# Linear attention and squared-ReLU FFN on one core: a new written-out issue order, W1 in eighths, transposes by TensorE or DMA chosen per unit

## The chip, the core and the metric

The kernel runs on one core of one Trainium2 chip. The metric is device time in microseconds (us); ten runs of the kernel before have a median of 180.53 us (179.64 to 183.67). The profile is that of one execution of 180.4 us, whose recorded span is 178.6 us. The engines are called PE (matrix engine), DVE (vector), ACT (scalar), POOL (GpSimd) and SP (the queue that issues most transfers).

## The reference

```python
# r, k, v: (4, 8, 768, 48) float32; w, u: (8, 48)
for t in range(S):
    cur = einsum('bhd,bhe->bhde', u * k[t], v[t])
    y[t] = einsum('bhd,bhde->bhe', r[t], state + cur)
    state = w[..., None] * state + einsum('bhd,bhe->bhde', k[t], v[t])
x = y.transpose(0, 2, 1, 3).reshape(3072, 384)
h = maximum(x @ w_in, 0)          # w_in: (384, 2048)
out = (h * h) @ w_out             # w_out: (2048, 384)
```

A decaying state per head and batch gives y, and all 3,072 tokens then go through a feed-forward layer whose hidden values are squared after the ReLU.

## The kernel before, in words

The sequence is cut into 24 *units* of 128 tokens; unit i is chunk i // 4 of batch i % 4. Units are taken together in 13 *groups* for the feed-forward layer: units 0 and 1 alone, then pairs (group 5 holds units 8 and 9, group 7 units 12 and 13).

Every operation is a *step* with a short name, a method of the class `Do`. A unit needs these:

- `ld` loads r, k and v as float32, from rows of 48 values (five buffers for each of r, k and v).
- `kh` and `rh` multiply k and r by powers of the decay (`Wkhat`, `Wt2`) into the bf16 tile `rk`; `vb` casts v to bf16. `P0`, `P1`, `du` and `dv` make the term of the current token: r * k, times u, summed over the head, times v.
- `rk` has to be transposed: `T` on PE into a PSUM bank and `Tc` that copies it out, or `XB`, one DMA transpose issued by SP. `A` multiplies the transposed tiles, `Bm` applies the causal mask while it moves the product out of PSUM.
- `Y` adds up the chunk's own part and the state's; `xs` moves it out of PSUM and adds `dv`. `U` makes the update of the state, `ts` and `S` (for the first chunks `S0`) apply it to `S0W`.
- `xs` has to be transposed as well: `X` on PE and `xTc`, or `xX`, a DMA transpose on SP.

A group then needs `F1` (eight steps per pair: 6 matmuls of 256 columns; for a single unit four steps of 12 matmuls of 128 columns), `re` (ReLU out of PSUM), `sq` (the square: form 0 on ACT, form 1 multiplies the PSUM bank by the ReLU's result, form 2 the result by itself out of SBUF), and per unit four `F2` steps of 4 matmuls of 384 columns, one for each quarter of W2. `os` evicts, `out` stores.

The weights: W1 is loaded in float32 quarters by SP (`lW`, L301) and cast to bf16 by `cW`; W2 comes in quarters by `W` (L317), a casting DMA issued by POOL. Ahead of each `W`, a `gate` (L311) copies one value of a v tile on POOL, so that the DMA is issued only after that tile has landed.

The string `ORDER` is the whole program: steps with their engine (A, D, G, P, S for ACT, DVE, POOL, PE, SP) and the buffers they take, worked out ahead of time and walked once by the loop at the end of the function. Each engine runs its steps strictly in that order, and waits where a step's input or buffer isn't ready. So the engine of a step, and its place among that engine's other steps, are what the string decides.

Of the kernel before, what the change touches and what calls it, by code (L numbers as in the profile page):

```python
# [29 lines left out]
sq.1.1:D2/3 ld.r.7:S/2 re.0.3:A/4 Bm.3.1:D/3 P0.3:G/3 F2.1.0:P/0 re.0.0:A/5 sq.0.3:D1/4 Y.2:P/0 ld.v.11:S/3  # L30
sq.0.0:A0/5 P0.4:G/1 F1.0.1:P/1 Bm.3.0:D/2 WLcol:A F2.0.0:P/1 xs.2:D/2 re.0.1:A/1 gate.1.3:G Y.3:P/2 W.1.3:G P1.3:D
X.2:P/0 sq.0.1:A0/6 F1.0.2:P/0 du.3:D/1 WLm:G xTc.2:A/0 re.0.2:A/0 F2.1.1:P dv.3:G S0.1:D sq.0.2:A0/7 U.3:P/0 S0.0:D
F2.0.1:P ld.r.6:S/3 rh.4:G xs.3:D/0 U.2:P/1 S0.3:D X.3:P/3 P1.4:G T.4:P/2 xTc.3:A S0.2:D F2.1.2:P Tc.4:A/4 kh.5:D/5
F1.2.1:P/1 du.4:D/0 F1.2.5:P/0 re.2.1:A/3 dv.4:G A.4:P/0/3 re.2.5:A/2 sq.2.1:D1/8 F2.0.2:P sq.2.5:A0/9 ld.k.10:S/4
kh.6:G/0 Bm.4.1:D/0 F2.1.3:P Bm.4.0:D/1 ld.v.5:S/4 F1.2.7:P/0 os.1:A/0 F1.2.3:P/1 ld.k.11:S/3 re.2.7:D/4 vb.9:A/5
Y.4:P/1 re.2.3:A/5 U.4:P/2 ld.v.6:S/1 rh.5:D F1.2.0:P/0 sq.2.3:A0/10 ts.4:D/0 P0.5:G/0 T.5:P/3 out.1:S sq.2.7:A0/11
xs.4:D/1 F1.2.6:P/1 S.4:G Tc.5:D/5 ld.r.9:S/4 re.2.0:A/1 X.4:P/0 F2.0.3:P sq.2.0:A0/12 re.2.6:D/0 ld.k.8:S/0 P1.5:G
A.5:P/2/1 vb.11:A/6 xTc.4:D/1 F2.2.0:P/0 ld.v.7:S/2 Bm.5.1:D/5 sq.2.6:A0/13 rh.6:G F1.2.4:P/0 os.0:A/1 du.5:D/2
ld.r.11:S/0 F1.2.2:P/1 Bm.5.0:D/4 re.2.4:A/3 kh.7:G/1 out.0:S F2.3.0:P/1 vb.5:A/7 re.2.2:D/2 T.6:P/3 dv.5:G
sq.2.4:D1/14 sq.2.2:A0/15 Y.5:P/0 U.5:P/1 Tc.6:A/0 F2.2.1:P rh.7:D ld.v.10:S/4 xs.5:D/2 P0.6:G/2 F2.2.2:P vb.6:A/0  # L40
ts.5:D/1 X.5:P/2 F2.2.3:P P0.7:G/3 ld.k.9:S/1 xTc.5:A ld.r.12:S/3 T.7:P/3 os.2:A/2 F1.3.1:P/1 P1.6:D ld.k.12:S/2
Tc.7:A/1 ld.r.8:S/2 F1.3.5:P/0 du.6:D/1 P1.7:G out.2:S re.3.1:D/5 vb.7:A/3 A.6:P/0/1 A.7:P/2/3 S.5:G re.3.5:A/4
du.7:D/0 F2.3.1:P sq.3.5:A0/16 Bm.6.0:D/2 F2.3.2:P dv.7:G sq.3.1:A0/17 Bm.6.1:D/3 F1.3.7:P/1 vb.10:A/1 Bm.7.0:D/1
kh.8:G/4 F1.3.0:P/0 ld.v.8:S/2 re.3.7:A/1 Y.6:P/0 sq.3.7:A0/18 dv.6:D F1.3.3:P/1 re.3.0:A/0 xs.6:D/0 kh.9:G/2
ld.v.12:S/1 U.6:P/1 F2.3.3:P re.3.3:D/3 sq.3.0:A0/19 X.6:P/2 rh.8:G F1.3.2:P/0 ts.6:D/0 os.3:A/0 sq.3.3:A0/20 out.3:S
F2.4.0:P/0 S.6:D XB.8:S/2 re.3.2:A/2 F1.3.4:P/1 Bm.7.1:D/0 P0.8:G/1 sq.3.2:A0/21 F1.3.6:P/0 re.3.4:D/4 xTc.6:A/0
P1.8:G F2.4.1:P ld.k.13:S/0 sq.3.4:D1/22 re.3.6:A/5 ld.r.13:S/2 Y.7:P/0 vb.8:A/4 sq.3.6:D1/23 rh.9:G F2.4.2:P
vb.12:A/2 xs.7:D/1 U.7:P/1 F2.4.3:P P0.9:G/0 XB.9:S/3 ts.7:D/1 X.7:P/3 F2.5.0:P/1 os.4:A/1 S.7:D xTc.7:A ld.k.14:S/1
F2.5.1:P out.4:S du.8:D/2 P1.9:G F1.4.5:P/1 ld.r.14:S/4 F1.4.1:P/0 dv.8:D re.4.5:A/1 F2.5.2:P du.9:D/1 kh.10:G/3
ld.v.13:S/2 sq.4.5:A0/24 F1.4.3:P/1 re.4.1:A/0 dv.9:D AA.8:P/2/0/1/3 sq.4.1:A0/25 rh.10:G re.4.3:D/3 ld.v.14:S/0  # L50
F1.4.4:P/0 Bm.8.0:D/4 sq.4.3:A0/26 F1.4.0:P/1 P0.10:G/2 XB.10:S/4 Bm.8.1:D/5 re.4.4:A/2 F2.5.3:P sq.4.4:A0/27
re.4.0:D/4 P1.10:G ld.k.15:S/4 Y.8:P/2 vb.13:A/7 ld.r.15:S/1 U.8:P/0 os.5:D/2 F1.4.7:P/0 sq.4.0:A0/2 kh.11:G/5
xs.8:D/2 out.5:S F1.4.2:P/1 re.4.7:A/5 ts.8:D/0 xX.8:S/1 F2.6.0:P/0 rh.11:G Bm.9.0:D/2 sq.4.7:A0/5 F1.4.6:P/0
re.4.2:A/1 Bm.9.1:D/3 S.8:G XB.11:S/5 F2.7.0:P/1 sq.4.2:A0/3 du.10:D/0 Y.9:P/2 re.4.6:A/0 dv.10:D U.9:P/0 F2.7.1:P
sq.4.6:A0/6 xs.9:D/0 P0.11:G/3 ld.v.15:S/4 F2.7.2:P ts.9:D/1 vb.14:A/0 xX.9:S F2.7.3:P P1.11:G ld.k.16:S/3 ld.r.16:S/0
F2.6.1:P os.7:D/0 S.9:G AA.10:P/1/3/2/0 du.11:D/2 out.7:S F2.6.2:P vb.15:A/3 dv.11:D F1.5.0:P/1 Bm.10.0:D/1 kh.12:G/0
ld.v.16:S/3 F1.5.1:P/0 Bm.10.1:D/0 re.5.0:A/3 rh.12:G F2.6.3:P Bm.11.0:D/4 re.5.1:A/2 Y.10:P/1 sq.5.0:D1/0 sq.5.1:A0/7
P0.12:G/1 XB.12:S/0 U.10:P/3 F1.5.2:P/0 os.6:A/1 xs.10:D/1 F1.5.3:P/1 P1.12:G vb.16:A/4 ld.k.17:S/2 ts.10:D/0 out.6:S
re.5.2:A/4 F2.8.0:P/1 Bm.11.1:D/5 xX.10:S/0 S.10:G re.5.3:A/5 F2.9.0:P/0 ld.r.17:S/3 sq.5.2:D1/1 sq.5.3:A0/4 Y.11:P/2
du.12:D/1 kh.13:G/1 U.11:P/1 F1.5.4:P/1 xs.11:D/2 F1.5.5:P/0 ts.11:D/1 rh.13:G re.5.4:A/1 F2.8.1:P re.5.5:A/0 dv.12:D  # L60
XB.13:S/1 F2.9.1:P sq.5.5:A0/12 xX.11:S S.11:G sq.5.4:D1/8 F1.5.6:P/0 ld.v.17:S/1 F1.5.7:P/1 P0.13:G/0 re.5.6:A/2
F2.8.2:P re.5.7:A/3 sq.5.6:D1/15 P1.13:G ld.k.18:S/0 F2.9.2:P sq.5.7:A0/10 ld.r.18:S/2 AA.12:P/3/0/2/1 kh.14:G/4
du.13:D/0 F2.8.3:P dv.13:D F1.6.0:P/1 vb.17:A/5 Bm.12.0:D/2 rh.14:G os.8:A/2 ld.v.18:S/2 F1.6.1:P/0 re.6.0:A/4 out.8:S
Bm.12.1:D/3 F2.9.3:P P0.14:G/2 re.6.1:A/5 XB.14:S/2 sq.6.0:D1/14 Y.12:P/3 os.9:A/0 U.12:P/0 F1.6.2:P/0 Bm.13.0:D/1
P1.14:G sq.6.1:A0/9 ld.k.19:S/1 out.9:S F1.6.3:P/1 xs.12:D/0 re.6.2:A/0 ld.r.19:S/4 kh.15:G/2 ts.12:D/0 F2.10.0:P/1
# [12 lines left out]
Bm.17.0:D/4 F2.13.2:P vb.21:A/7 sq.8.0:D1/27 Y.16:P/1 re.8.1:A/3 P1.18:G ld.k.23:S/0 U.16:P/3 F2.13.3:P ld.r.23:S/2
sq.8.1:A0/24 xs.16:D/1 kh.19:G/1 F1.8.2:P/0 ts.16:D/0 vb.22:A/0 xX.16:S/1 Bm.17.1:D/5 os.13:A/1 F1.8.3:P/1 S.16:G
# [443 lines left out]
```

## Time and profile before

| | |
|---|---|
| median of ten runs | 180.53 us |
| profiled execution, and its span | 180.4 us, 178.6 us |
| PE, DVE, ACT, POOL busy | 157.6, 124.8, 119.9, 113.9 us |
| F1 matmuls (L433), F2 matmuls (L460) | 74.5 us busy, 73.3 us busy |
| one load of r, k or v | 192 KB, 3.7 to 4.0 us from issue to landing |
| one quarter of W2 | 7.7 us from issue to landing |
| one transpose by DMA of rk, of xs | 3.4 us, 3.1 us from issue to landing |

Busy time is the union over an engine's instructions, so overlapping matmuls aren't counted twice. A group's row has its number of instructions, their busy time, the mean of one, and the idle time of the engine ahead of them with what ended it. The chain of waits is followed back from the last instruction, and shows which work or wait set the end.

### The profile page before, as it was taken

Reading aid. Unit: us, or ns where it says so; the run is one execution under the profiler, and the core shown is the slowest. Engines: PE = TensorE matmul, PEld = TensorE weight load, DVE = VectorE, ACT = ScalarE, POOL = GpSimd, SP = SyncE. Lnnn points to the kernel's source line nnn. Section 1 sums busy time; section 2 is a strip of 40 time slices with the busy share of each in tenths; the row PEclk is TensorE's granted clock in tenths of the full one; section 3 lists DMA queues with packets and bytes.
Section 4 is the critical chain, followed back from the end, with each engine's and each line's share of the span. In section 5 each row is a group of like instructions: output and inputs, shape, how many; then the busy total and the mean of one; then the engine's idle time right before and its main releaser. Section 6 shows DMA issues by size and latency. Waiting matters only on the chain.

```text
span 178.6 us, 4254 instructions
## 1 busy us (share of the span) xinstructions
PE 157.6 (88%) x1640; PEld 119.3 (67%) x1640; DVE 124.8 (70%) x220; ACT 119.9 (67%) x209; POOL 113.9 (64%) x125
## 2 busy tenths in 40 slices
PE   0142789999999999979999989999999999999992
PEld 0031778678768778648778668677777777777761
DVE  3678389969987979687669787688993796713310
ACT  2373469778778768727757759577777676587851
POOL 3508688947966998895898978969989920000000
PEclk9999999999999999999999999999999999999999
DMA  5999999989999799999899999899634442220102
GB/s 116 257 372 200 221 248 213 217 150 212 215 230 224 169 228 165 223 183 201 173 186 163 213 210 180 147 235 188 134 87 112 103 79 72 70 66 21 49 22 88
DMA packets 106052, 29.66 MB, mean 166 GB/s; under 512 B 99368, under 2 KB 104496, under 8 KB 106032
## 3 DMA queue, kind: packets, MB, share of 16 engines
q1 hardware_dynamic: 103912, 27.81, 73.7%
q0 software_dynamic: 2112, 1.57, 5.7%
q8 instruction: 13, 0.21, 0.5%
q14 instruction: 7, 0.06, 0.1%
q10 hardware_dynamic: 8, 0.01, 0.0%
HBM read 20.46 MB, written 4.72 MB: 141 GB/s over the span
## 4 chain that ended last, share of the span: by engine, by line
PE 59%; DMA 14%; SPq 14%; DVE 4%; issue 3%; POOL 3%; ACT 2%; ACTq 0%
PE bank L433 26%; PE bank L460 26%; SPq L296 9%; DMA ldv<-in_v_dram 9%; DMA W<-in_moe_w_out_dram 5%; PE bank L360 2%; SPq L424 2%; PE bank L382 1%; PE bank L380 1%; SPq L301 1%; POOL S0W L412 1%; PE bank L391 1%; DVE Bm L372 1%; ACT hr L441 1%; SPq L353 1%
## 5 line engine op out<-in xcount | busy, mean ns | idle before, releaser
L433 PE MATMUL bank<-xT,W 128*128 128x256 bf16 (+1 forms) x624 | 74.5, 270 | 2.7 <-ACT hr L441 0.8
L460 PE MATMUL bank<-W,hq 128*128 128x384 bf16 x384 | 73.3, 326 | 0.6 <-DMA W<-in_moe_w_out_dram 0.4
L433 PEld LDWEIGHTS <-W 128*128 128x128 bf16 x624 | 57.6, 100 | 13.3 <-issue 2.2
L441 ACT ACTIVATE hr<-bank 128x512 bf16<-128x512 f32 x86 | 50.7, 595 | 23.2 <-PE bank L433 21.9
L460 PEld LDWEIGHTS <-hq 128*128 128x128 bf16 x384 | 36.2, 98 | 19.0 <-issue 0.9
L450 DVE TENSOR_TENSOR hq<-bank,hr 128x512 bf16<-128x512 f32 x37 | 25.4, 688 | 27.3 <-ACT hr L441 27.1
L448 ACT ACTIVATE hq<-hr 128x512 bf16<-128x512 bf16 x57 | 35.7, 630 | 2.3 <-DVE hr L443 0.7
L372 DVE TENSOR_TENSOR Bm<-bank,maskJT 128x512 bf16<-128x512 f32 x48 | 31.0, 681 | 1.8 <-PE bank L360 1.5
L326 POOL TENSOR_TENSOR P<-ldr,ldk 128x384 f32<-128x384 f32 x22 | 23.7, 1080 | 2.4 <-DMA ldr<-in_r_dram 2.3
L320 POOL TENSOR_TENSOR rk<-ldk,Wkhat 128x384 bf16<-128x384 f32 x21 | 21.8, 1042 | 4.0 <-ACT Wkhat L274 4.0
L330 POOL TENSOR_TENSOR P<-P,ub 128x384 f32<-128x384 f32 x20 | 21.9, 1095 | 1.2
L323 POOL TENSOR_TENSOR rk<-ldr,Wt 128x384 bf16<-128x384 f32 x20 | 21.6, 1081 | 1.4 <-DMA ldr<-in_r_dram 1.4
L412 POOL TENSOR_TENSOR S0W<-ts,WLm 128x384 bf16<-128x384 f32 x14 | 14.5, 1035 | 9.8 <-DVE ts L409 9.8
L250 ACT CAST vb<-ldv 128x384 bf16<-128x384 f32 x22 | 11.1, 507 | 12.7 <-DMA ldv<-in_v_dram 12.7
L399 DVE TENSOR_TENSOR xs<-bank,dv 128x384 bf16<-128x384 f32 x24 | 13.2, 552 | 5.1 <-PE bank L382 4.1
L250 ACT COPY os<-bank 128x384 f32<-128x384 f32 x22 | 10.4, 474 | 7.6 <-PE bank L460 7.4
L338 DVE TENSOR_TENSOR dv<-ldv,du 128x384 f32<-128x384 f32 x19 | 14.1, 741 | 0.3
L347 PE MATMUL bank<-identity,rk 128*128 128x128 bf16 x64 | 6.3, 253 | 8.6 <-POOL rk L320 7.5
L382 PE MATMUL bank<-vb,Bm 128*128 128x48 bf16 x192 | 11.5, 186 | 2.6 <-DVE Bm L372 2.6
L333 DVE TENSOR_REDUCE du<-P 128x8 f32<-128x384 f32 x24 | 13.0, 544 | 0.2
L382 PEld LDWEIGHTS <-Bm 128*128 128x128 bf16 x192 | 9.9, 98 | 4.1 <-DVE Bm L372 2.9
L347 PEld LDWEIGHTS <-rk 128*128 128x128 bf16 x64 | 5.0, 115 | 9.3 <-POOL rk L320 7.5
(57 smaller groups left out, 115.9 us busy)
## 6 DMA issues: line engine op xcount, KB each, us to landing
ldk<-in_k_dram SPq DMA_DIRECT2D x24, 192.0 KB, 3.8
ldr<-in_r_dram SPq DMA_DIRECT2D x24, 192.0 KB, 3.7
ldv<-in_v_dram SPq DMA_DIRECT2D x24, 192.0 KB, 4.0
out_dram<-os SPq DMA_DIRECT2D x24, 192.0 KB, 2.6
ws<-in_moe_w_in_dram SPq DMA_DIRECT2D x4, 768.0 KB, 6.8
W<-in_moe_w_out_dram POOLq DMA_DIRECT2D x4, 384.0 KB, 7.7
rkT<-rk SPq DMA_TRANSPOSE x16, 3.4
xT<-xs SPq DMA_TRANSPOSE x16, 3.1
```

The source lines that it names most:

```text
L250: e.copy(o, a)
L320: e.tensor_mul(rk[slot[f"rk{i}"]][:, 1, :, 0:D], loaded("k", i), Wkhat)
L323: e.tensor_mul(rk[slot[f"rk{i}"]][:, 0, :, 0:D], loaded("r", i), Wt2)
L326: e.tensor_mul(P0b[slot[f"P{i}"]], loaded("r", i), loaded("k", i))
L330: e.tensor_mul(t, t, ub)
L372: e.tensor_mul(Bmb[slot[f"Bm{i}{h}"]], heads(bank(f"bA{i}{h}"), 128), mask_b)
L382: e.matmul(y[:, hc, D * h : D * (h + 1)], m[h][:, hc, :], vb[:, 2 * hc + h, :], start=(c == 0), stop=True, skip_group_check=True,)
L433: e.matmul(hp[:, fi, :], W1[f // 4][:, c, 128 * (f % 4) : 128 * (f % 4 + 1)], xt[:, c, :], start=(c == 0), stop=(c == CCH - 1), skip_group ...
L441: e.activation(hr, hp, AF.Relu)
L448: e.activation(hq, hr, AF.Square)
L450: e.tensor_mul(hq, bank(f"bH{g},{s}", "bH"), hr)
L460: e.matmul(bank(f"bO{i}", "bO")[:, 0:d_model], hqb[slot[f"hq{g},{f // m}"]][:, at : at + L], W2[q][:, f % 4, :], start=(f == 0), stop=(f = ...
```

## The change

The string `ORDER` is replaced by another. The steps are nearly the same, but their engines and places aren't:

| step | before | after |
|---|---|---|
| kh | DVE 3, POOL 21 | DVE 19, POOL 5 |
| rh | DVE 4, POOL 20 | DVE 14, POOL 10 |
| P0 / P1 | DVE 2 / 4, POOL 22 / 20 | DVE 12 / 12, POOL 12 / 12 |
| dv | DVE 19, POOL 5 | DVE 9, POOL 15 |
| S | DVE 2, POOL 14 | DVE 10, POOL 6 |
| vb | ACT 22, DVE 1, POOL 1 | ACT 14, DVE 4, POOL 6 |
| re | ACT 86, DVE 10 | ACT 72, DVE 24 |
| sq, forms 0 / 1 / 2 | 57 / 37 / 2 | 61 / 1 / 34 |
| os | ACT 22, DVE 2 | ACT 15, DVE 9 |
| T with Tc / XB | 8 / 16 | 9 / 15 |
| X with xTc / xX | 8 / 16 | 10 / 14 |
| xTc | ACT 6, DVE 2 | ACT 5, DVE 5 |

Before, the units with T and X are 0 to 7; after, T serves 0 to 8 and X serves 0 to 9. W1 is held in eighths of 256 columns: five are loaded by SP and cast by ACT (3) and POOL (2), three come by a casting DMA that POOL issues, as W2's quarters do. The gates go, dv and xs have four buffers in place of three, and hq 32 in place of 28. The step `AA`, two `A` in a row, goes; its uses are two `A` steps. A step `Z` is defined but not used.

```diff
-POOLS = dict(ldr=5, ldk=5, ldv=5, ws=4, rk=6, P0=4, dv=3, vb=8, rkT=6, bank=4, bankH=2, bankO=2, Bm=6, xs=3, xT1=2, xT2=2, xT4=1, hr=6, hq=28, os=3, ts=2)
-GATES = [[('v', 1), ('v', 1), ('v', 1), ('v', 1)], [('v', 1), ('v', 1), ('v', 3), ('v', 3)]]
+POOLS = dict(ldr=5, ldk=5, ldv=5, ws=0, wsa=4, rk=6, P0=4, dv=4, vb=8, rkT=6, bank=4, bankH=2, bankO=2, Bm=6, xs=4, xT1=2, xT2=2, xT4=1, hr=6, hq=32, os=3, ts=2)
 ORDER = """
-tab:A ld.k.1:S/0 ld.r.0:S/0 ld.r.1:S/1 ld.k.0:S/1 w:A lW.0.2:S/0 u:S lW.0.0:S/1 lW.0.1:S/2 ld.v.1:S/0 shw:D ld.k.2:S/2
-logw:A Wk:A ld.v.3:S/1 P0.1:D/0 Wt:A kh.1:G/0 ld.r.2:S/2 kh.0:D/1 rh.1:D rh.0:G ld.k.4:S/3 T.1:P/0 cW.0.2:A ld.v.4:S/2
...
-kh.22:G/3 du.21:D/1 F2.16.2:P re.9.7:A/4 sq.9.6:D1/13 AA.20:P/3/0/2/1 sq.9.7:A0/11 rh.22:G F1.10.0:P/1 dv.21:D
-F2.16.3:P XB.22:S/4 re.10.0:A/0 Bm.20.0:D/4 P0.22:G/2 F1.10.1:P/0 os.16:A/1 Bm.20.1:D/5 F2.17.1:P out.16:S re.10.1:A/1
...
+w:A ld.r.0:S/0 u:S tab:A ld.k.0:S/0 ld.r.1:S/1 ld.k.1:S/1 ld.r.3:S/2 shw:D ld.k.3:S/2 ld.k.2:S/3 logw:A ld.r.2:S/3
+Wk:A ld.v.1:S/0 Wt:A kh.0:D/0 lW.0.7:S/0 P0.0:D/0 shu:D rh.0:G ld.v.0:S/1 P1.0:D T.0:P/0 lW.0.6:S/1 kh.1:D/1 Tc.0:A/0
+du.0:D/0 lW.0.0:S/2 P0.1:D/1 rh.1:D lW.0.1:S/3 kh.3:D/2 T.1:P/1 P1.1:D A.0:P/2/3 ld.v.3:S/2 Tc.1:A/1 rh.3:D kh.2:D/3
+ld.v.2:S/3 Bm.0.0:D/0 P0.2:G/2 A.1:P/0/1 du.1:D/1 T.3:P/2 P0.3:G/3 Bm.1.1:D/1 Tc.3:A/2 rh.2:D cW.0.7:A dv.0:G
+Bm.1.0:D/2 A.3:P/1/2 Bm.0.1:D/3 vb.1:A/0 T.2:P/0 dv.1:G lW.0.4:S/0 vb.0:A/1 Bm.3.0:D/4 wc:S Y.1:P/3 Tc.2:A/3 P1.2:G
+Bm.3.1:D/5 Y.0:P/1 ld.k.4:S/4 xs.1:D/0 cW.0.6:A P1.3:G ld.r.4:S/4 A.2:P/2/0 xs.0:D/1 ld.k.5:S/0 X.1:P/3 Bm.2.0:D/1
+xTc.1:A/0 W.0.5:G X.0:P/1 cW.0.0:A Bm.2.1:D/2 F1.1.3:P/0 ld.r.5:S/0 cW.0.1:G ld.v.4:S/4 xTc.0:D/1 du.2:D/2 re.1.3:A/0
+F1.1.0:P/1 du.3:D/3 ld.v.5:S/0 vb.3:A/2 dv.2:G vb.2:A/3 F1.0.0:P/0 re.1.0:D/1 dv.3:G Y.2:P/3 U.1:P/2 re.0.0:A/2
+Y.3:P/0 xs.2:D/2 F1.0.3:P/1 ld.k.7:S/1 sq.1.0:A0/0 cW.0.4:G xs.3:D/3 X.2:P/1 U.2:P/3 re.0.3:D/3 W.0.2:G X.3:P/0
+xTc.2:A/0 F1.0.2:P/0 ld.k.6:S/3 WLcol:A sq.0.3:D2/1 F1.1.2:P/1 xTc.3:D WLm:G re.0.2:A/4 ld.r.6:S/1 U.0:P/1 W.0.3:G
+kh.4:D/4 re.1.2:A/5 F1.2.6:P/0 ld.r.7:S/2 sq.1.3:A0/2 rh.4:D F1.2.4:P/1 re.2.6:A/1 P0.4:D/0 T.4:P/0 ld.k.10:S/2 S0.1:D
+re.2.4:A/3 P1.4:G F1.2.0:P/0 Tc.4:D/4 sq.2.4:A0/3 F1.2.7:P/1 W.1.0:G kh.5:D/5 re.2.0:A/0 A.4:P/2/0 S0.2:D re.2.7:A/3
+W.1.1:G F1.2.2:P/0 sq.2.6:D2/4 sq.0.0:A0/5 S0.0:D F1.2.1:P/1 W.1.2:G sq.0.2:D2/6 re.2.2:A/1 ld.k.8:S/4 rh.5:D U.3:P/3
+sq.2.0:A0/7 F1.0.1:P/0 Bm.4.0:D/0 P0.5:G/1 re.2.1:A/2 ld.v.8:S/1 Bm.4.1:D/3 T.5:P/1 re.0.1:A/4 W.1.3:G F1.1.1:P/1
...
+F2.1.0:P/0 xs.4:D/0 re.2.3:A/4 F2.0.0:P/1 du.5:D/0 sq.1.1:A0/9 Bm.5.1:D/2 ld.k.9:S/0 X.4:P/0 vb.5:A/5 dv.5:G U.4:P/2
...
+XB.15:S/2 Bm.13.0:D/4 sq.5.2:A0/6 ld.r.17:S/4 P1.15:G U.13:P/2 F2.8.0:P/0 out.7:S du.13:D/1 re.5.6:A/5 rh.14:D
+F2.9.0:P/1 sq.5.6:A0/12 Bm.12.1:D/3 dv.13:G re.5.7:A/3 F1.6.0:P/1 XB.14:S/3 kh.16:D/0 sq.5.7:A0/2 ld.v.14:S/4 F2.9.1:P
+P1.14:G re.6.0:D/0 sq.5.5:A0/1 F1.6.3:P/0 du.15:D/3 Y.12:P/1 P0.19:G/3 du.14:D/2 F1.6.1:P/1 sq.6.0:D2/7 U.11:P/0
...
-    wsb = bufs("ws", [128, 1536], FP32)
+    wsb = {"wsa": bufs("wsa", [128, CCH, 256], FP32), "ws": bufs("ws", [128, 4, d_model], FP32)}
...
-    W1 = [const.tile([128, CCH, 512], BF16, name=f"W1_{s}") for s in range(4)]
+    W1 = [const.tile([128, CCH, 256], BF16, name=f"W1_{s}") for s in range(FCH // 2)]
...
+    def weights(a, s):
+        return w_out_t[:, 4 * s : 4 * s + 4, :] if a else w_in_t[:, :, 256 * s : 256 * (s + 1)]
...
         def lW(e, a, s):
-            t = wsb[slot[f"ws{a}{s}"]]
-            if a == 0:
-                e.dma_start(out=t.rearrange("p (c f) -> p c f", c=CCH), in_=w_in_t[:, :, 512 * s : 512 * (s + 1)])
-            else:
-                e.dma_start(out=t.rearrange("p (f o) -> p f o", f=4), in_=w_out_t[:, 4 * s : 4 * s + 4, :])
+            e.dma_start(out=wsb[("wsa", "ws")[a]][slot[f"ws{a}{s}"]], in_=weights(a, s))
...
-        def gate(e, a, s):
-            x, i = GATES[a][s]
-            e.tensor_copy(gate[:, 4 * a + s : 4 * a + s + 1], loaded(x, i)[0:1, 0, 0:1])
         def W(e, a, s):
...
+            e.dma_start(out=(W1, W2)[a][s], in_=weights(a, s))
...
-        def AA(e, i):
-            Do.A(e, i)
-            Do.A(e, i + 1)
...
-                        hp[:, fi, :], W1[f // 4][:, c, 128 * (f % 4) : 128 * (f % 4 + 1)], xt[:, c, :],
+                        hp[:, fi, :], W1[f // 2][:, c, 128 * (f % 2) : 128 * (f % 2 + 1)], xt[:, c, :],
```

## The prediction

> **What bounds the kernel now.** I read the busy shares and slices first. The matrix engine (PE) is busy for 157.6 of 178.6 us, and its empty slices lie in the first 36 us; the transfer engines are full for the first two thirds.
>
> ```profile
> PE 157.6 (88%) x1640; PEld 119.3 (67%) x1640; DVE 124.8 (70%) x220; ACT 119.9 (67%) x209; POOL 113.9 (64%) x125
> ...
> PE   0142789999999999979999989999999999999992
> ...
> DMA  5999999989999799999899999899634442220102
> ```
>
> The table by stretches comes next: stretch and its length in us, busy time of PE, PE's weight loads, DVE, ACT and POOL, granted clock, busy share of the 16 DMA engines, GB/s.
>
> ```profile
> 0.00:44.00 44.00, 28.32 (x333) 22.42 (x335) 31.84 (x65) 27.18 (x42) 27.04 (x41) 1.00 1.03 220
> 44.00:93.00 49.00, 47.75 (x506) 35.65 (x506) 39.43 (x66) 34.16 (x64) 41.13 (x41) 1.00 0.97 199
> 93.00:133.00 40.00, 39.24 (x429) 30.07 (x427) 33.26 (x57) 28.63 (x53) 35.11 (x35) 1.00 0.95 177
> 133.00:179.00 46.00, 42.30 (x379) 31.18 (x376) 20.25 (x34) 29.96 (x53) 10.66 (x11) 1.00 0.26 68
> ```
>
> Until 133 us the DMA share is 0.95 to 1.03, and until 133 us DVE and POOL are loaded too; only the last 46 us belong to PE alone. The chain of waits gives the pace of PE, and the wait that ends the start:
>
> ```profile
> 27.11 8.57 DMA W<-in_moe_w_out_dram
> 35.73 0.81 PE bank L460 x4
> ...
> 50.62 0.45 PE bank L347 x8
> 51.07 1.31 PE bank L433 x12
> ...
> 56.85 0.65 PE bank L460 x4
> 57.50 0.17 PE bank L417 x3
> ```
>
> A useful measure is the *lag*: the time at which PE reaches a step, less the PE work issued ahead of it. At such spacings the whole program is 96 F1 steps (0.655) + 96 F2 (0.65) + 24 A (0.275) + Y (4 of 0.20, 20 of 0.37) + 20 U (0.17) + 8 T (0.45) + 8 X (0.17) = 148.6 us. By the starts of each unit's last F2 matmul in the trace, the lag is 22.3 us at unit 0 (43.7 us), 24.6 at unit 9 (92.9), 26.1 at unit 15 (133.0) and 26.4 at the end (175.0). Span = 148.6 + 26.4 + 3.6 (last eviction, store) = 178.6. A changed kernel is worth what it does to the lag.
>
> What sets it? Pricing transfers by the trace's packet records as time of all 16 engines: a load of r, k or v (1,024 packets of 192 B, 16 ns each) 1.03 us, XB (1,024 of 256 B, 23 ns) 1.47, xX (384) 0.55, a quarter of W1 2.3, of W2 2.55, an output store 0.57. Added up in order, 79.3 us of transfers are issued up to xX.9, which the F1 steps of group 5 need, with 54.3 us of PE work ahead of them: a lag of 25.0, against 24.6 measured there. For XB.19 it is 123.1 - 100.1 = 23.1. So W2's arrival sets the first 22 us and the transfer queue the rest.
>
> **The change part by part.**
>
> *PE.* One more T and two more X: +0.45 + 2 x 0.17 = +0.8 us, all of it on the path: 149.4.
>
> *Transfers.* One XB and two xX fewer: -1.47 - 1.1. W1 is now five staged eighths on SP and three cast eighths on POOL's queue in place of four quarters on SP (9.2). No row shows these packet sizes. An eighth staged has 384 packets of 1,024 B, between 0.55 us (256 B at 23 ns) and 1.7 (1,536 B at 71 ns); I take 1.2, by size nearer the second. A cast one (512 B) lies between 0.55 and 1.9 (768 B at 80 ns); I take 1.6. W1 becomes 10.8, from 4.4 to 14.2. Total 139.6 -> 138.6. The new order's worst point is xX.13 ahead of group 7's F1: 100.3 of transfers against 76.3 of PE work, a lag of 24.0 (24.6 and 25.0 before); XB.19 gives 22.6, xX.15 22.9. Transfers alone therefore give some 2 us back; with W1 at its bounds the lag would be 17.6 or 27.4.
>
> *The start.* F2 comes later in the order: 17.5 us of PE work stand before it (8.0 now). W2's issues stand on POOL behind the first units' work. dv.0 needs v.0, the tenth load (11.5 us of transfers, landing about 3 later: 14.5). From there POOL has 4 dv (0.83), 3 P1 (1.0), 3 W.0 issues (0.82), 2 eighths to cast (half of 1.46), WLm (1.1): 11.4 us, and about 1 of waits. So W2's quarters are issued from 27 to 31 us and land 8.6 later, 36 to 40. With 22.5 and 25.7 us of PE work ahead of the third and the fourth quarter, this wait falls from a lag of 22.3 to about 15. What is late next: the transfers (about 20 for W2 in their sum, 24 later) and the vector engine. The four gate copies (1.1 us of POOL) held W2 back behind loads; with them gone W2 competes with the loads, inside the same sum.
>
> *ACT and POOL.* ACT loses 14 relus, 7 evictions and 8 casts and gains 4 squares: 120 -> 106. POOL drops 52 operations of 1.0 us and takes on 10 dv (0.83), 5 casts (0.5) and 3 issues (0.82): 105 -> 67. Neither is a bound before or after, so this is worth nothing by itself.
>
> *DVE.* It takes that work. Back to back, an operation costs its duration less 0.08: two P1 (0.55 each) take 1.03, four Bm (0.68) 2.48. So P0 +10, P1 +8 at 0.475: +8.6; kh +16: +7.6; rh +10, S +8 at 0.48: +8.6; os +7: +3.4; re +14 at 0.61: +8.5; vb, xTc +3 each: +1.9; dv -10: -4.8; squares from PSUM -36 at 0.61, from SBUF +32 at 0.33: -11.4. Sum +22.4: DVE's plain work goes from 110 to 132 us, nearly all before PE's last 30 us.
>
> And 114 of DVE's operations (37 before) now read both inputs from SBUF. The trace shows what these do beside POOL:
>
> ```profile
> 7.39 1.31 POOL L323 TENSOR_TENSOR rk<-ldr,Wt 128x384 bf16<-128x384 f32 x1
> ...
> 7.78 1.34 DVE L323 TENSOR_TENSOR rk<-ldr,Wt 128x384 bf16<-128x384 f32 x1
> 9.04 0.54 DVE L326 TENSOR_TENSOR P<-ldr,ldk 128x384 f32<-128x384 f32 x1
> ```
>
> ```profile
> L338 DVE TENSOR_TENSOR dv<-ldv,du x19: 545/643/1357, 16.8 to 147.7; 128x384 f32<-128x384 f32 x19
> ```
>
> ```profile
> L372 DVE TENSOR_TENSOR Bm<-bank,maskJT x48: 673/680/692, 14.0 to 153.4; 128x512 bf16<-128x512 f32 x48
> ```
>
> The rh on DVE ends 0.42 us after POOL's ends; without POOL the same shape takes 0.54. dv runs from 545 to 1357 ns, while Bm, with one input in PSUM, stays at 673 to 692 whatever POOL does. The square from SBUF took 411 ns once and 1,214 once. The 37 now lose 7.5 us in all (dv 3.6, rh 2.1, kh 0.7, squares 0.8, S 0.3): 0.20 each, with POOL 64% busy. In the changed kernel POOL is about half as busy, which would give 0.15; but DVE, 80 to 90% busy with such operations, is hit by nearly every POOL operation, as rh was (0.5 each). Lower end 0 (order keeps them apart), upper 0.30; I take 0.20.
>
> Lag by DVE: up to Bm.19, 101.7 us of plain DVE work and 90 such operations stand against 101.8 of PE work. Add 6.4 us before the first kh (Wkhat is done at 6.35 now) and about 2 of early waits: 8.3 + 90 x 0.20 = 26.3; with 0.15 21.8, with 0.30 35.3. Before, the same sum is -9 + 8: DVE was free.
>
> *The sum.* Transfers give 24.0, DVE 26.3: two queues, each strictly in order, nearly equal, each feeding the other (XB and xX wait in SP's queue for kh, rh and xs, of which DVE now makes most; kh waits for loads). Now DVE waits 27.1 us for ACT relus in its squares alone (25 times, 2.3 at most) and can afford it. I add 1.5. Lag 27.8. Span 149.4 + 27.8 + 3.6 = 180.8; the profiled run's 180.4 has 1.8 around its span: 182.6; the median is 0.1 above that run: 182.8, 1.2% slower.
>
> The Trainium skill, "SBUF — State Buffer", section "Who interferes with whom", says that a Vector instruction with two SBUF inputs contends with a GpSimd instruction reading SBUF, that the second to issue fully blocks for the whole instruction, and that one SBUF input doesn't contend: the three rows above agree. Read as a rule against this change, half of 114 operations would meet a POOL operation of 1.0 us with half of it left, 0.25 each; my estimate from that page is a lag of 30.8 + 1.5 and 187.3 us; by the row's 0.20 it is 182.8.
>
> **The rivals.**
> - *Transfers decide, DVE keeps up.* If the order keeps two-input operations and POOL's apart (below 0.17 each, DVE's lag stays under 24), xX.13 sets a lag of 24.0 to 24.3: 149.4 + 24.2 + 3.6 + 1.8 = 179.0, and 178.0 with staged eighths of W1 at 1.0. For it: 52 of POOL's 97 operations of 1.0 us leave, and PE waits less for W2. Against it: the 0.20 measured. This one is faster.
> - *Gain and loss cancel.* W2's wait is gone, DVE's takes its place at a lag of 25 to 26: 179.8 to 181.2. At 0.17 to 0.19 per operation.
> - *POOL and DVE alternate.* Every POOL operation delays DVE by what is left of it (0.30 per DVE operation): lag 35.3 + 1.5, 191.6. For it: rh's rows (564 to 1,464 ns). Against it: the P1 rows on DVE stayed at 541 to 559 with POOL at work.
>
> **How the numbers follow.** The measurement tells 0.5% from no change, 0.9 us. Forecast (181.4 to 187) 0.41, alternating (above 187) 0.18, cancelling 0.14, transfers decide 0.27. So slower 0.59, same 0.14, faster 0.27. The range 177.6 to 191.5 leaves out about 1 in 20 below and 3 in 20 above; the forecast's own range is 181.4 to 187.
>
> **What would show it.** DVE busy at 145 us or more, its SBUF squares far above 411 ns in the mean (600 or so), kh, rh and dv likewise; Bm still 680. PE's lag at unit 0's F2 below 21 and growing to 27 or more by unit 15; PE waiting for DVE's Bm, xs and squares rather than for loads of v; POOL's busy time near 70 us; the DMA share still near 1 until 110 us. If squares stay near 411 ns, the DVE step is wrong and the time falls below 180. If PE's first stage is no shorter, the W2 step is wrong.

## The result, and the profile after

The changed kernel takes 183.9 us in the median of 15 runs; the kernel before took 181.8 us beside it, in the median of 52. The ratio is 1.0133, with a 95% interval of 1.0102 to 1.0165: slower by 1.3%. The kernel before itself had medians of 181.1 to 183.6 us in the sessions below, so everything is compared by its ratio to the kernel before in the same session. On 180.53 us, the median that the prediction started from, the ratio gives 182.9 us; 182.8 was forecast.

The profile read here is that of the second run of the changed kernel (183.45 us, span 181.7 us); the first one (span 183.7 us) and that of the experiment "stores early" fell into slower, disturbed executions, and their spans are not compared. First the busy shares and slices:

```profile
PE 160.5 (88%) x1654; PEld 120.8 (66%) x1654; DVE 146.5 (81%) x285; ACT 101.8 (56%) x184; POOL 75.4 (42%) x88
...
PE   0256999599999999998976999999999999999992
...
PEclk9999999999999999999997899999999999999999
...
DMA  2999999999998999998899997996365320230032
```

Work has moved to DVE (124.8 us before), and away from ACT (119.9) and POOL (113.9). PE has a dip just past the middle, with a lower granted clock behind it. By stretches (length, busy time of PE, its weight loads, DVE, ACT and POOL, granted clock, share of the transfer engines, GB/s):

```profile
0.00:44.00 44.00, 30.31 (x373) 24.97 (x374) 36.07 (x75) 25.39 (x43) 24.15 (x37) 1.00 1.04 198
44.00:93.00 49.00, 47.77 (x502) 35.00 (x501) 47.09 (x88) 33.20 (x61) 27.71 (x27) 1.00 1.00 188
93.00:133.00 40.00, 37.05 (x389) 27.78 (x388) 34.87 (x68) 21.46 (x40) 19.57 (x20) 0.96 0.82 176
```

DVE is busy for 47.1 of the 49 us from 44 to 93, and the transfers are full as well. PE has gained 2 us in the first stretch (28.3 before) and lost 2 in the third (39.2 before).

The operations on DVE that the prediction spoke of, each with number and shortest, median and longest duration in ns:

```profile
L439 DVE TENSOR_TENSOR hq<-hr x34: 407/419/1202, 25.5 to 173.4; 128x512 bf16<-128x512 bf16 x34
```

```profile
L359 DVE TENSOR_TENSOR Bm<-bank,maskJT x48: 674/680/693, 12.6 to 151.6; 128x512 bf16<-128x512 f32 x48
```

Squares from SBUF run up to 1,202 ns, but the median is close to the shortest; their mean is 506. `Bm`, with one input in PSUM, is as before.

The chain of waits in the stretch where the time is lost:

```profile
81.75 3.02 DMA ldv<-in_v_dram
...
89.01 2.04 SPq L344
91.06 0.05 issue
91.11 0.57 SPq L299
91.69 0.04 issue
91.78 4.17 DMA out_dram<-os
96.03 0.10 ACT os L250
96.12 0.28 issue
96.40 0.61 ACT hr L428
97.06 0.82 PE bank L420 x6
```

PE stood still from 94.1 to 97.1 us for a ReLU on ACT, which stood behind the eviction os.9, which waited for a store (out.7) to leave its buffer, and this store had been issued late on SP.

### The profile page after: what moved, and what is told of

Its sections match the earlier page's. It is cut to its first block, busy times and chain, and to the rows that moved or that the text cites. A ratio compares the mean times of both kernels' runs of the same rounds, so it can differ in the third digit from the quotient of the medians.

```text
span 183.7 us, 4288 instructions
## 1 busy us (share of the span) xinstructions
PE 161.1 (88%) x1654; PEld 121.3 (66%) x1654; DVE 148.9 (81%) x285; ACT 102.1 (56%) x184; POOL 75.0 (41%) x88
## 4 chain that ended last, share of the span: by engine, by line
PE 72%; DVE 12%; DMA 7%; ACT 3%; issue 3%; POOL 1%; SPq 1%; POOLq 0%; DVEq 0%; ACTq 0%
PE bank L447 30%; PE bank L420 30%; PE bank L351 4%; DVE Bm L359 2%; DMA out_dram<-os 2%; DMA ldr<-in_r_dram 2%; PE bank L369 2%; DVE rk L314 2%; PE bank L338 2%; DMA ldv<-in_v_dram 2%; PE bank L378 2%; DMA ldk<-in_k_dram 2%; PE bank L367 2%; DVE hq L439 2%; ACT rkT L250 1%
## 5 line engine op out<-in xcount | busy, mean ns | idle before, releaser
L428 ACT ACTIVATE hr<-bank 128x512 bf16<-128x512 f32 x72 | 42.2, 595 | 36.7 <-PE bank L420 35.9
L447 PEld LDWEIGHTS <-hq 128*128 128x128 bf16 x384 | 36.2, 98 | 19.1 <-issue 0.9
L430 DVE TENSOR_SCALAR hr<-bank 128x512 bf16<-128x512 f32 x24 | 16.2, 684 | 11.6 <-PE bank L420 9.6
L329 POOL TENSOR_TENSOR dv<-ldv,du 128x384 f32<-128x384 f32 x15 | 13.5, 908 | 19.3 <-DVE du L324 18.9
L439 DVE TENSOR_TENSOR hq<-hr 128x512 bf16<-128x512 bf16 x34 | 17.3, 520 | 2.0 <-ACT hr L428 1.9
L314 POOL TENSOR_TENSOR rk<-ldr,Wt 128x384 bf16<-128x384 f32 x10 | 11.1, 1110 | 16.1 <-DMA ldr<-in_r_dram 12.5
L317 POOL TENSOR_TENSOR P<-ldr,ldk 128x384 f32<-128x384 f32 x12 | 13.7, 1149 | 8.7 <-DMA ldr<-in_r_dram 7.0
L311 DVE TENSOR_TENSOR rk<-ldk,Wkhat 128x384 bf16<-128x384 f32 x19 | 12.8, 680 | 1.9 <-DMA ldk<-in_k_dram 1.9
L321 POOL TENSOR_TENSOR P<-P,ub 128x384 f32<-128x384 f32 x12 | 12.9, 1083 | 2.1 <-DVE P L317 2.1
L250 ACT COPY rkT<-bank 128x1024 bf16<-128x1024 bf16 x8 | 8.1, 1011 | 9.0 <-PE bank L338 8.8
L351 PE MATMUL bank<-rkT 48*128 48x128 bf16 x192 | 9.7, 240 | 2.3 <-ACT rkT L250 2.1
```

Of the source, the lines that this page charges most:

```text
L250: e.copy(o, a)
L314: e.tensor_mul(rk[slot[f"rk{i}"]][:, 0, :, 0:D], loaded("r", i), Wt2)
L351: e.matmul(heads(bank(f"bA{i}{h}"), 128)[:, hc, :], t[p0 : p0 + D, HP + hc, :], t[p0 : p0 + D, hc, :], start=True, stop=True, skip_group_c ...
L428: e.activation(hr, hp, AF.Relu)
L430: e.tensor_scalar_max(hr, hp, 0.0)
L439: e.tensor_mul(hq, hr, hr)
```

## The experiments

The lag is the prediction's: the time at which PE reaches a unit's last F2, less the PE work ahead of it. By the prediction's spacings, with 0.30 us for a single `A` and 0.55 for a pair in one step, the changed order holds 149.8 us of PE work, so that the span is 149.8 + lag at the end + 3.6 (149.8 + 28.2 + 3.6 = 181.6; measured 181.7). Of the 149.8, 0.4 is a matter of counting: ten `A` follow an `A` at 0.23 us in the traces of both kernels, though only the order before calls some of them a pair. With the 149.4 of the prediction the lag at the end is 28.6. These are the profiled executions, in order of the text:

| run | ratio to before | lag at unit 0 | unit 9 | unit 11 | end |
|---|---|---|---|---|---|
| the kernel before | 1 | 22.2 | 24.5 | 24.8 | 26.3 |
| the changed kernel again | 1.0122 | 20.6 | 22.9 | 27.7 | 28.2 |
| POOL reads nothing | 0.997 | 18.4 | 23.2 | 27.6 | 28.3 |
| ReLU on ACT | 1.007 | 21.7 | 23.6 | 26.7 | 29.1 |
| stores early | 1.0109 | not compared | | | |
| eight output buffers | 1.0155 | 20.6 | 23.3 | 25.6 | 27.5 |
| before, eight output buffers | 0.9987 | 22.2 | 24.0 | 24.3 | 26.8 |
| eight buffers, POOL reads nothing | 1.0007 | 17.1 | 21.5 | 25.3 | 25.6 |
| eight buffers, ReLU on ACT | none | 20.3 | 22.1 | 26.1 | 26.7 |
| urgent transfers first | 1.013 | 21.3 | 23.8 | 24.8 | 31.1 |
| urgent transfers, ReLU on ACT | 1.0064 | 19.7 | 22.5 | 23.7 | 28.1 |
| before, squares from SBUF | 1.0016 | 22.7 | 28.0 | 28.4 | 30.3 |
| light v loads | 0.9832 | 20.6 | 22.8 | 23.0 | 23.4 |

The ratio is the median over many runs, the lag is that of one; where they disagree (POOL reads nothing) the ratio counts. Not every profiled execution is typical: that of the changed kernel is the fastest of its ten (183.45 us, median 185.37), that of light v loads the fastest of its four (178.67, median 179.69), and the one with urgent transfers first lies above its median (186.35, 185.40). Lags of two runs can thus differ by a microsecond or two without a cause in the edit.

**The changed kernel again**, in another session.

> The changed kernel once more, for a profile at full clock: the first one has a granted clock of 0.87 between 100 and 110 us, just after PE stood still from 96.0 to 98.6. Theory D (DVE paces, as predicted): lag about 21 at unit 0's last F2, then growing steadily to 27 or more by unit 15, in small waits. Theory S (a store holds the queues up): the lag is near 24 until unit 6 and jumps by 2.5 or more within 85 to 100 us, where ACT's eviction of unit 9 waits for the landing of unit 7's store. In both the ratio to before is 1.010 to 1.017.

Measured 1.0122 (1.0069 to 1.0175). The result stands.

**POOL reads nothing.** POOL's arithmetic is replaced by operations of about the same length (0.17 for each value read, 0.41 for each write of zeros) that read single values in place of tiles; the order is the same.

```diff
+    def quiet(e, o, ins, n):
+        for a in ins:
+            e.tensor_copy(seen1, a)
+        for _ in range(n):
+            e.memset(o, 0.0)
...
         def kh(e, i):
+            if e is nc.gpsimd:
+                return quiet(e, rk[slot[f"rk{i}"]][:, 1, :, 0:D], [one("k", i)], 2)
             e.tensor_mul(rk[slot[f"rk{i}"]][:, 1, :, 0:D], loaded("k", i), Wkhat)
```

> The changed kernel in which POOL's arithmetic (kh, rh, P0, P1, dv, S, vb where they are POOL's) is left out: POOL reads one value of each input, to keep the waits, and writes zeros over the whole output, about as long as before. So DVE's operations with two SBUF inputs find no POOL operation that reads whole tiles. Theory D by blocking: the 13 us by which these 114 operations exceed their shortest go (DVE busy 149 to 137, squares from 520 to about 420 ns in the mean) and the time falls by 2 to 4 us, ratio to before 0.99 to 1.003. Theory S, and a rival in which DVE's blocked time is off the path: less than 1 us, ratio 1.008 to 1.015.

Measured 0.997 (0.9929 to 1.0012), 1.5% below the changed kernel in the same session. POOL stays 69.1 us busy, yet DVE's operations no longer stretch: the squares' row, and one example from the changed kernel for comparison, first POOL's timeline, then DVE's (start, duration, line, operation):

```profile
L464 DVE TENSOR_TENSOR hq<-hr x34: 408/417/426, 25.1 to 173.4; 128x512 bf16<-128x512 bf16 x34
```

```profile
31.11 1.03 POOL L317 TENSOR_TENSOR P<-ldr,ldk 128x384 f32<-128x384 f32 x1
```

```profile
31.23 1.20 DVE L439 TENSOR_TENSOR hq<-hr 128x512 bf16<-128x512 bf16 x1
```

POOL's P0 ended at 32.14, the square at 32.43. This holds nearly throughout the trace: a DVE operation with two inputs in SBUF that starts while POOL computes lasts what is left of POOL's operation plus 0.281 us (square) or 0.414 us (128x384 in float32). In the changed kernel 26 of 110 such operations started with more than 0.14 us of a POOL operation left; 23 of them follow the rule to within 10 ns. In the other three it was POOL that waited, though the trace has it starting 0.04 to 0.31 us earlier: DVE's operation took its usual 0.55 us, and POOL's ended 0.86 us behind it. The 110 lost 10.4 us (0.09 each; 0.12 in the first profile; the prediction had counted 114). The rule leaves one long operation unexplained, a square of 0.75 us at 30.09 that met only POOL's issues of W2. The Trainium skill, "SBUF — State Buffer", section "Who interferes with whom", states the lock that these rows show: the second to issue waits for the whole of the first, and a GpSimd instruction that only writes SBUF doesn't take part, as here.

So POOL's reads cost the kernel about 2.7 us, and DVE's loss of 10 us mostly doesn't reach the end. The edit shortens POOL's busy time as well (from 75.4 us to 69.1, since its operations no longer wait for DVE's), and the kernel before wasn't run with it. How much of the 2.7 us comes from DVE's waiting alone, and how much of it is the changed kernel's own, isn't shown.

**ReLU on ACT.** 24 steps `re` and 9 steps `os` go from DVE to ACT.

```diff
-... re.1.0:D/1 ... re.0.3:D/3 ... os.0:D/1 ...
+... re.1.0:A/1 ... re.0.3:A/3 ... os.0:A/1 ...
```

> The changed kernel with DVE's 24 ReLUs and 9 evictions moved to ACT at the same places of the order: DVE loses 24 x 0.61 + 9 x 0.48 = 19 us of plain work, ACT goes from 102 to about 121 busy. Theory D by plain work: 2 us or more faster than the changed kernel, ratio to before below 1.003. Theory S: the eviction that waits still holds ACT up, with more ReLUs behind it; no gain or slower, ratio 1.010 to 1.03.

Measured 1.007 (1.0024 to 1.0116), with DVE at 132.7 us and ACT at 117.3. That is 0.5% below the changed kernel, with intervals that overlap. 14 us less work on DVE bring 1 us: DVE's amount of work isn't the whole answer either.

**Stores early.** 15 of the 24 stores were moved to eight steps behind their eviction, so that the eviction three further on finds its buffer free.

```diff
-... os.7:A/0 ... (38 steps) ... out.7:S
+... os.7:A/0 ... (8 steps) ... out.7:S
```

> The changed kernel with 15 output stores moved forward in SP's order, to 8 steps behind their own eviction (they stand 20 to 238 behind it). Nothing else is moved. Theory S: the wait of ACT for a free output buffer (4.7 us) and PE's pause behind it (2.6 us) go; 2.5 to 4 us faster than the changed kernel, a ratio to before of 0.993 to 1.003. Theory D: DVE's queue takes the place of that wait, less than 1 us is gained, ratio 1.007 to 1.015. Third: SP now waits for evictions ahead of loads, and it gets slower.

Measured 1.0109 (1.0068 to 1.015): no gain. In its profile SP, which waits strictly in order, stood for out.6 until ACT had evicted, and so r of unit 17 landed late; DVE's rh.17 and all behind it waited. That this is what used up the gain in the other executions too isn't shown:

```profile
94.84 0.61 ACT hr L428
95.44 0.17 SPq L462
95.62 0.05 issue
95.67 3.77 DMA ldr<-in_r_dram
99.44 0.02 issue
99.47 0.04 DVE rk L314
```

**Eight output buffers.** This takes away what os.9 waits for and moves nothing.

```diff
-POOLS = dict(... os=3, ts=2)
+POOLS = dict(... os=8, ts=2)
-... os.2:A/1 ... os.5:D/0 ... os.4:D/2 ... os.7:A/0 ...
+... os.2:A/3 ... os.5:D/4 ... os.4:D/5 ... os.7:A/6 ...
```

> The changed kernel with eight output buffers in place of three; the order of all steps is the same, only an eviction no longer waits for the store of the third output before it. Nothing is left out. Theory S (the eviction os.9, held 4.7 to 5.1 us on ACT by the landing of out.7, makes PE's pause of 2.6 to 3.0 us at 94 to 97 us, and the half clock after it, 1.7 us): os.9 starts at once, PE's lag stays near 24 to 25 at unit 11 instead of 27.7 to 29.2, and the ratio to the kernel before is 0.985 to 0.997. Theory D (DVE, blocked by POOL, is late there in any case and takes the pause's place): the lag at unit 11 falls by 1 us at most, ratio 1.006 to 1.012.

The kernel before with eight buffers is the control:

> The kernel before with eight output buffers, order unchanged, nothing left out: a control. Its evictions show no such wait on PE's path; both theories expect 0.997 to 1.003. If this gains as much as the changed kernel gains by its eight buffers, the buffers don't explain the difference of the two kernels.

Measured 1.0155 (1.0111 to 1.0198), and 0.9987 (0.9952 to 1.0022) for the control. Theory S, that the store's wait cost 2.6 to 3 us and the slow clock after it, is wrong: nothing was gained. In the profiled executions the lag at unit 11 fell by 2.1 us (27.7 to 25.6), more than theory D allowed, but it was back at 27.4 by unit 15. The changed kernel's own timeline shows why, once the other engines' rows are read beside the chain (in brackets, the idle time before the instruction and what ended it):

```profile
95.55 0.56 DVE L314 TENSOR_TENSOR rk<-ldr,Wt 128x384 bf16<-128x384 f32 x1 [2.85 <-DMA ldr<-in_r_dram]
...
96.03 0.48 ACT L250 COPY os<-bank 128x384 f32<-128x384 f32 x1 [5.09 <-DMA out_dram<-os]
...
97.06 0.82 PE L420 MATMUL bank<-xT,W 128*128 128x256 bf16 x6 [2.95 <-ACT hr L428]
```

Two waits ended within half a microsecond: ACT's for the store, and DVE's for r of unit 17. Both transfers had been issued by SP one after the other, behind the transpose XB.15. With the first wait gone, the second one takes over, and then the transpose of `xs`; the chain of the run with eight buffers:

```profile
88.45 1.67 SPq L344
90.12 0.05 issue
90.18 4.64 DMA ldr<-in_r_dram
94.81 0.02 issue
94.84 0.04 DVE rk L314
...
96.67 0.47 DVE xs L386
...
98.88 0.01 DVE P L317
98.90 3.09 DMA xT<-xs
101.98 0.14 issue
102.12 0.46 PE bank L420 x3
```

**Eight buffers, POOL reads nothing.** Both edits together.

> The changed kernel with eight output buffers, and POOL's kh, rh, P0, P1, dv, vb and S left out: for each of them POOL reads one value of the inputs and writes zeros, at the same place in the order. Theory S alone: the same time as with eight buffers alone, within 0.5%. Theory D alone: the same as with three buffers (ratio 0.997). Both causes, one behind the other: the gains add up, some 1.5% here and what eight buffers give by themselves, a ratio of 0.975 to 0.99.

Measured 1.0007 (0.9969 to 1.0045). Against eight buffers alone the gain is again 1.5% (2.7 us); against three buffers with the same edit, none. The gains don't add, since the buffers had none.

**Eight buffers, ReLU on ACT.**

> The changed kernel with eight output buffers, and the 24 ReLUs and 9 evictions of DVE given to ACT, at the same places in the order; nothing is left out. DVE's plain work falls from about 147 to 133 us, as in the run with three buffers (ratio 1.007). If DVE's amount of work is what is late, this is 1% or more below eight buffers alone, with the lag at unit 15 at 25 or less; if ACT's queue (held by evictions and ReLUs that wait for PE) is as late as DVE's, no change within 0.5%.

The median of six runs is 182.28 us, 0.8 below eight buffers alone and 1.2 above the kernel before. One run of the six took 179.17 us and the others 182.0 to 182.6, so no interval can be given and the question is not settled by this run. Its chain, up to 40 us, names the wait for W2, issued at 29.70 and landing 10.41 later, at which PE's lag is 20.3.

**Urgent transfers first.** If SP's order is what is late, transfers that aren't needed for 20 to 40 us can stand back. With eight output buffers, seven loads change places: r of unit 17 goes forward, six others back.

```diff
-xX.11 ... ld.r.18 ... ld.k.18 ... XB.15 ld.r.17 out.7 XB.14 ... ld.v.20 ld.k.20 ld.v.22 xX.13 ... ld.r.23 ... xX.14 ... xX.15
+xX.11 ld.r.17 ... XB.15 out.7 ld.r.18 XB.14 ld.k.18 ... xX.13 ld.k.20 ... xX.14 ld.r.23 ... xX.15 ld.v.20 ... ld.v.22
```

> The changed kernel with eight output buffers and eight of SP's transfers in other places: ld.r.17 behind xX.11 (four loads earlier), and ld.r.18, ld.k.18, ld.k.20, ld.v.20, ld.v.22 and ld.r.23, which are used 20 to 40 us after their landing, behind the transfers that PE waits for (XB.14, XB.15, xX.13, xX.14, xX.15). Nothing is left out. In the run with eight buffers ld.r.17 landed at 94.8 us and held rh.17 and with it DVE's queue, and xX.13, which stood behind ld.v.20, ld.k.20 and ld.v.22, landed at 102.0 us and held PE. Theory T (the order on SP's queue sets PE's lag between 93 and 103 us): the lag at unit 11 falls from 25.6 to 23.3 to 24.2, the end from 27.5 to below 26, and the ratio to the kernel before is 0.995 to 1.008, against 1.0155 with eight buffers alone. Theory D (DVE is late there by itself): the lag at unit 11 stays above 25, ratio 1.010 or more.

and with the ReLUs on ACT as well:

> The kernel of the run above with the 24 ReLUs and 9 evictions of DVE given to ACT as well; nothing is left out. If SP's order and DVE's amount of work both hold PE, one behind the other, the gains add up: 0.5% below the run above or more, a ratio of 0.985 to 1.000, and the lag at unit 15 near 24. If one replaces the other, no change against the run above within 0.5%.

Measured 1.013 (1.0086 to 1.0175) and 1.0064 (1.0016 to 1.0112). The lag at unit 11 fell, from 25.6 to 24.8 (and to 23.7 with the ReLUs moved): the wait for xX.13 went, as theory T said, though by less than it said. Then it came back 20 us later, where the transfers that had been put off stood ahead of another transpose:

```profile
115.92 0.58 SPq L299
116.50 0.04 issue
116.55 1.34 SPq L299
117.89 0.04 issue
117.93 4.74 DMA rkT<-rk
122.67 0.05 issue
122.72 0.40 PE bank L351 x8
```

This is A.19 waiting for XB.19. The two loads shown (k of unit 23, v of unit 21) are in their old places; v of units 20 and 22, which had been put off, were issued ahead of them, at 111.2 and 112.5 us. This new order moved the wait instead of removing it. Neither kernel beats the one before. The ReLUs on ACT give 0.66% here, with intervals that again overlap.

**Before, squares from SBUF.** One part of the change alone: 37 squares of the kernel before read the ReLU's result twice in place of the bank.

```diff
-... sq.0.3:D1/4 ... sq.2.1:D1/8 ...
+... sq.0.3:D2/4 ... sq.2.1:D2/8 ...
```

> The kernel before with its 37 squares on DVE taken from SBUF (the ReLU's result by itself) in place of the PSUM bank; one part of the change alone, nothing is left out, and POOL stays 64% busy. Unblocked, such a square takes 0.41 us, 0.28 less than from PSUM. By the prediction's price (0.20 lost per operation with two inputs in SBUF) the 37 take 0.61 us in the mean; if POOL's operations block for all that is left of them (0.30 or more), 0.71 or more; if the loss is 0.115 as in the changed kernel, 0.53. DVE has slack in this kernel, so PE's time should hardly move: ratio 0.995 to 1.005; at 1.01 or more even this kernel's DVE can't afford it.

```profile
L452 DVE TENSOR_TENSOR hq<-hr x39: 408/468/1273, 26.6 to 175.4; 128x512 bf16<-128x512 bf16 x39
```

The mean is 688 ns, which is a loss of 0.27 each, as much as the square saves against PSUM (0.688 there too). The ratio is 1.0016 (0.9957 to 1.0075). Beside a POOL that is 64% busy, 41 of 73 operations with two SBUF inputs met one of POOL's; in the changed kernel, where POOL is 42% busy, 26 of 110 did.

**Light v loads.** The loads of v of units 8 to 23 bring one head of eight; eight output buffers.

```diff
         def ld(e, x, i):
+            if x == "v" and i >= 8:
+                return e.dma_start(out=loaded(x, i)[:, 0:1, :], in_=single[x][i % B, i // B][:, 0:1, :])
             e.dma_start(out=loaded(x, i), in_=single[x][i % B, i // B])
```

> The changed kernel with eight output buffers, in which the loads of v of units 8 to 23 bring only the first of eight heads (128 packets in place of 1,024); seven eighths of those 16 loads are left out, and all steps that use v work on what is in the buffer. This takes 16 x 0.9 = 14 us of time of the transfer engines away. If the transfers set PE's lag behind unit 8 (25.6 at unit 11, 27.5 at the end), it falls back to what the start gave, 22 to 23.5, and the ratio is 0.985 to 0.995. If DVE sets it, it stays above 25 and the ratio above 1.005.

Measured 0.9832 (0.9782 to 0.9882), 3.2% below eight buffers alone, below even the range given for the transfers. The lag stays at 22.7 to 23.4 from unit 5 to the end. The table by stretches:

```profile
44.00:93.00 49.00, 47.43 (x508) 35.52 (x506) 47.60 (x89) 34.47 (x65) 28.05 (x27) 1.00 0.92 175
93.00:133.00 40.00, 39.90 (x436) 30.52 (x433) 38.16 (x77) 22.89 (x43) 22.58 (x22) 1.00 0.72 148
```

DVE does the same work, blocked by the same POOL, at 97% busy, and PE loses 0.1 us in 40. With 14 us less of transfers DVE keeps up. The kernel before wasn't run with light loads either, so how much of this gain is the changed kernel's own is open.

## Why the prediction was right, and where its reasons were not

The time, the sign and the size came out: 1.2% slower forecast, 1.33% measured, a lag of 27.8 forecast and 28.2 measured, in an execution that was the fastest of its ten. That the sum held is in part luck: two of its terms were wrong in opposite directions. By the prediction's own conditions a loss below 0.17 us per operation, which is what came, meant a faster kernel of 179.0. (Two slips alter nothing: the operations with two SBUF inputs are 110 and 36, not 114 and 37, and its terms add up to 182.7.)

*The price of blocking was too high.* The prediction had 0.20 us per operation with two SBUF inputs, though POOL would be half as busy, because DVE, when almost always busy, would be "hit by nearly every POOL operation". It measured 0.09 to 0.12. The rule for one meeting was right; the number of meetings wasn't. It was lower beside a less busy POOL: 17 of 36 met before, 26 of 110 after. 0.20 was right for the kernel before (0.21 by this count), and adding 37 squares there cost 0.27 each. The lower value that the prediction set aside, 0.15, was nearer. The squares' mean was 506 ns, not 600.

*DVE's own lag was too high with it.* Forecast 26.3. With 0.09 to 0.12 in place of 0.20 the prediction's formula gives 16.4 to 19.1. With the transfers lightened, the lag with all of DVE's blocking is 23.4, so DVE's own is no more than that. The row that the prediction named as its test, squares near 411 ns, came out between (median 419, mean 506); the inference drawn from it, a time below 180, didn't follow, because of the next term.

*What the two queues cost each other was too low.* The prediction added 1.5 us for it, to the larger of the two. With DVE's term as measured, the larger is the transfers' 24.0, and about 4 us are missing up to 28.2. With eight buffers the lag ends at 27.5; without POOL's reads at 25.6, of which 1.7 is a stretch of slow clock (below) that the other two runs don't have; with light loads at 23.4. By these lags both queues in place are 2 to 4 us above either one relieved; by the ratios the reliefs gained 1.5% (2.7 us) and 3.2% (5.9 us). The chain shows the mechanism it named: r waits in SP's queue, rh waits for r, xs waits behind rh on DVE, xX waits for xs and for SP, PE waits for xX.

*Transfers.* By the trace the packets took 140.3 us of all 16 engines (143.2 before), against 138.6 (139.6) worked out. A staged eighth of W1 took 1.24 (1.2 forecast), a cast one 1.51 (1.6). The worst point, xX.13 with a lag of 24.0, is where the run with eight buffers waits (102.0 us). Of the two reliefs tried, which aren't equal in size, that of the queue that the prediction put second gained more.

*The start.* The lag at unit 0 fell below 21, to 20.6, and DVE is what the chain names there (squares and rh stretched by POOL, 1.12 and 1.89 us); without POOL's reads it is 17.1 to 18.4. But W2's limit is 18 to 20, not 15: its quarters were issued from 28.8 to 32.1 (27 to 31 forecast) and landed 6.1, 7.9, 9.8 and 10.9 us later, where the prediction had 8.6 for each. In this trace PE came to each quarter 2.7 us or more after it had landed. Without POOL's reads PE took the second and the fourth quarter within 0.05 us of their landing (37.88 and 44.28), at a lag of 18.4; with eight buffers and the ReLUs on ACT it waited for the first and the second, at 20.3. The prediction had looked at the third and the fourth.

*PE, ACT, POOL.* PE's work is 149.8 by the count above (149.4 forecast); DVE 146.5 busy (145 or more), ACT 101.8 (106), POOL 75.4 (70). That ACT and POOL gained nothing held.

*The rivals.* "POOL and DVE alternate" is out: 26 of 110 meet. "Transfers decide, DVE keeps up" had its condition met, a loss below 0.17 us, and its time wrong, 179.0, since it let the two queues run side by side for nothing. "Gain and loss cancel" holds only with POOL's reads left out (0.997 and 1.0007).

Two things stay open. Neither relief was tried on the kernel before, so the runs show what holds the changed kernel up, and not how much of that is new with it. And it isn't known whether DVE or the transfers would be the limit if each were lightened by the same share: the edits aren't equal, POOL's reads cost DVE 10 us, the light loads spare the transfers 14.

## What to carry to other kernels

Price an engine lock by two factors, the cost of one meeting and the chance of one: the first was the same to within 10 ns in 23 of 26 meetings here and can be read from a stretched row, the second was lower where the other engine was less busy (26 of 110 beside a POOL busy for 42%, 41 of 73 beside one busy for 64%), so a price from one kernel doesn't carry over to one with another share. When two queues, each strictly in order, come out within a few microseconds of each other, and each waits for the other's results, don't take the larger: here both together were 2 to 4 us worse than with either relieved. And before a wait in the chain is called the cause, read what the other engines were waiting for at that time: another wait that ends half a microsecond earlier will take its place.

## What the runs showed of the hardware

Eight of the fourteen profiled executions have, ahead of their end, a stretch of 3.41 us (one of 6.83) at half the granted clock; the kernel before's has none. In the 3.41 us just ahead of it PE was busy for 14 to 52% of the time in all eight. In the changed kernel it starts 1.0 us after PE's pause of 3.0 us ended:

```profile
93.00:97.00 4.00, 1.10 (x17) 0.68 (x16) 1.45 (x4) 0.97 (x3) 0.00 (x0) 1.00 1.01 225
97.00:98.00 1.00, 0.94 (x8) 0.78 (x8) 1.00 (x3) 0.91 (x4) 0.00 (x0) 1.00 1.05 245
98.00:101.50 3.50, 3.50 (x27) 1.88 (x25) 2.77 (x5) 2.00 (x4) 3.34 (x4) 0.51 0.91 194
101.50:105.00 3.50, 3.50 (x40) 2.98 (x39) 2.27 (x5) 2.20 (x4) 1.44 (x2) 1.00 0.88 194
```

It costs about 1.7 us, by an estimate (half of 3.4). One long pause isn't needed: with eight buffers and without POOL's reads it came at 96.2 us, with no pause above 0.8 us in the ten microseconds ahead of it; and it did not come behind a pause of 2.0 us with urgent transfers and ReLUs on ACT. The mean clocks of the timed runs show it in runs of both kernels, but more often in the changed one (nine of ten below 0.995 in the session of "the changed kernel again", ten of 31 of the kernel before), so it may be a part of the loss. It isn't all of it: with eight buffers the three runs at 0.997 or above have a median of 182.97 us, 1.0% above the 181.09 of the kernel before, whose 23 runs were all at 0.997 or above.

A DMA transpose holds SP's queue longer than a load does: after the first 20 us, XB took 1.3 us of it in the median (1.2 to 2.4), a load 0.6 to 0.8, in both kernels. And between 20 and 125 us SP had no gap above 1.3 us in the profiles of the kernel before and of the changed kernel again: nearly all the time it issued, or waited inside an issue.
